# A new order table for block-sparse attention and a GELU MLP: loads in a fixed order, SyncE counted as held by its DMA ring, outputs from SyncE or GpSimd

## The chip, the cores and the metric

The kernel runs on one core of one Trainium2 chip. The metric is device time in microseconds for one execution, and a smaller number is better. The core has TensorE (matrix products, called PE in the profile), VectorE (DVE), ScalarE (ACT), GpSimd (POOL) and SyncE (SP). Each takes its own instructions in order; semaphores tie them together. SyncE computes nothing: it issues DMAs. Each DMA it issues here stands in the profile as an "SPq" instruction, whose length is the time SyncE was held by it.

## What is computed

For each of 4 batches and 8 heads, 768 queries of width 64 attend to keys in blocks of 64. A query picks 3 blocks by the product with the mean key of each block, and its own block, under a causal mask. The heads of a batch are then put side by side and go through a two-layer MLP with GELU.

```python
k_rep = k.reshape(B, H, n_blocks, 64, D).mean(axis=3)
gate_scores = np.einsum('bhsd,bhnd->bhsn', q, k_rep)        # causal blocks only
top_idx = np.argsort(gate_scores, axis=-1)[..., -3:]         # plus the own block
scores = scale * np.matmul(q, k.transpose(0, 1, 3, 2))       # masked to those, causal
attn = np.exp(scores) / np.sum(np.exp(scores), axis=-1)      # in short
x = np.matmul(attn, v)      # heads side by side: [3072, 512]
h = x @ w_in                # [512, 2048]
out = gelu_tanh(h) @ w_out  # [2048, 512]
```

## The kernel before

**Work.** Two heads of a batch make a pair, so there are 16 pairs, p = 0 to 15, and 4 pairs to a batch b. For each pair the kernel loads q, k and v (named q5, k5, v5 for pair 5), turns q and k, computes the gate, selects blocks with ten maximum instructions (`sel_e`), and turns the selection into a mask. The scores of a pair are made in six or seven units, written (pair, unit): a score product (`st_e`) into one of two wide PSUM buffers, an exponential on ScalarE (`ex_e`), a causal select on GpSimd (`af_e`), and a product with v (`pv_e`). A norm (`zr_e`) and a transpose (`ot_e` on TensorE, or `otd_e` by DMA) follow. When the four pairs of a batch are done, `s1` makes the first MLP product in 16 strips f with GELU, and `s2` the second in 6 output tiles ti of 16 matmuls each; `cp_e` copies a tile out of PSUM to one of four buffers (`NOSB`), and `out_e` sends it to memory. A tile that reuses a buffer waits until the tile four before it has landed. The second product of one batch is interleaved with the attention of the next.

**Order.** Nothing is scheduled on the chip. Each piece is an `Op` made with `add`: the engines it can run on with assumed times, a function that emits it, and what it depends on. `ORDER` (line 22) is a table, written out by hand or by a search, of the numbers of these operations in the order in which they are placed; a letter behind a number picks the engine where there is a choice. `Plan.place` (line 165) goes through it and gives each operation a planned start; the instructions are then emitted in the order of these starts. So on each engine, the order of the table is the order of the program. The assumed times decide nothing else. `Plan.spare` (line 200) puts spare matmuls with a zero tile into holes of the planned TensorE time (`zero_mm`, line 1276).

**Loads.** `load_half` (line 371) loads the first pair's q and k in halves, two DMAs each (line 378). `load` (line 328) loads the others: as two DMAs (line 346), or, for q and k from pair 4 on, as four in another layout (line 355) which VectorE then turns. q and k have four buffers each and v three, so k4 takes the buffer of k0. A small copy `keep` (line 1304) reads k0 late, and so holds k4 back. `load_w` (line 573) casts the weights while they are loaded, by GpSimd: w_in in two parts, once v2 is there, and w_out in one, once k4, q4 and k5 are there. Before the issue it copies one element of each of these loads (line 582), which makes it wait for them. Mask transposes by DMA (`mask_d`, line 838), transposes of attention outputs (`otd_e`, line 1159) and all outputs (`out_e`, line 1255) but half of the last tile stand in SyncE's queue together with the loads.

Of the kernel before, what the change touches and what calls it, by code (L numbers as in the profile page):

```python
# [15 lines left out]
HOLD = 0  # L16
MASKVAL = 28672.0
# [5 lines left out]
1 2A 13 9 15 0 30 8 31D 6 161 3 288A 5 10 12 26 16 18 39 19 21 27 32 33 40 34  # L23
43 14 59 92 56 61 94 22 89 95 125 57 62 122 58 24 44A 41A 28A 38D 76 77A 53 29
54 42 45 52 78 35 36A 160 51A 80A 37 162 46 47 48 49D 7 109 165 166 167 25 163
66 79 91 169 170 97 50 55 70 173 177 68A 75 128 307 127 64 124 310 130 309 312
67 71 72 110D 81 82 83 73A 174 178 74 69 111 113A 183 99 168 180 101A 184 181
100 190 171 84 287 175 164 85 103 117 112 86D 192 193 194 289 65 98 108 102 87
88 214 185 142 176 204 104 186 105 106D 143D 114 215 205 200 172 179 196 182
144 145 201 197 146A 115 116 191 208 187 107 118 132 119D 211 221 198 202 131  # L30
206 155 156 159 120 121 209 212 136 195 223 199 203 213 231 141 133 137 138
134D 139A 140 224 147 227 232 216 207 245 210 228 242 148 149 246 243 151 235
135 217 152D 218 153 229 225 150 233 236 237 157 188 239 226 230 222 252 240
154 158 254 255 219 258 259 260 256 303G 304 313 306 234 262 238 266 244 241
263 267 264 268 316 292D 248 189D 575 578D 220D 273 247 257 249 270 265 261 274
279 276 253 285 622 519 625 682 679 571 628 271 277 269 250 275 281 272 251D
278 354 355 339 280 283 284D 282A 356 357 340 341 342 315 322 358 343 286 317
384 385 386 387 624 521 627 388 334 335 336 337 394 395 396 397 338 374 375 376
377 398 523 524 580 528 344 345 346 347 378 348 318 319 320 321 323 379 380 381
382 576 527 579 4 349 350 351 352 581 582 533G 383 359 529 353 360 361 362 369  # L40
370 371 372 363 373 534G 530 583 531 532 296D 577D 324 325 326 327 328 329 330
331 332 364 535 333 525D 584 526A 365 366 367 389 368 390 391 392 393 537D 587
290 561 399 400 401 402 403 404 405 406 407 408 409 410 411 536D 545 588D 589D
538 539 632 634D 633 412 413 414 415D 636 635D 541 562 546 417 419 549 550 420
553 421 422 423 424 425 426 427 522 551 552 428 554 586A 291 547 301 555 557
637 684 681 590 573 429 558 585A 559 293 294 540 542 563 295 543 297 430 431
432 433 569 434 435A 437 548 638 439 440 639 694 640 641 591 441 592 593 600
560 442 443 444 445 604 446 447 601 605 544 612 556 564 448 449 450 596 451 452
453 689 642A 613 454 608 300D 690 693 643G 594 614 574 597 455A 609 630 644 940
937 645 646A 647A 457 459 460 461 462 463 695 692D 565 696 697 698 606 602 464  # L50
465 466 467 468 469 603 470 595 598 599 298 299 610 699G 631 657 658 620 942
939 701 685 702 687 648 471 653 654 655 616 566 472 473 474 611 669 570 691D
952 475D 703D 477 670 479 480 661 607 481 482 649 662 659 650 671 651 483 656
665 484 485 615 677 666 621 302 714 715 660 486 706 487 707 652 488 710 711
700G 947 617 704D 667 663 673 948 705 489 664 668 722 490 491 726 708 688 712
723 724 716 727 728 951 492 672 493 674 718 678 719 734 720 995 997 567 436 308
943 416 93 63 618 568 418 945 713 494 953 709 495A 497 742 717 729 725 721 735
499 500 501 502 503 504 505 1005 730 731 732 949D 733D 740 1008A 1006 954 675
456 998 619 676 736 737 738 506 739 1000 507 743 508 744 745 741 746 747 509
748 749 750 751 950A 757 758 759 760 761 957D 1010 1009 958G 1007D 812 1011 955  # L60
813 814 815 777 778 779 780 816 781 807 808 809 810 767 768 769 770 811 787 788
789 790 771 762 763 764 765 791 766 797 798 799 800 792 793 794 795 801 752 753
754 755 796 756 772 773 774 775 776 782 783 784 785 786 802 803 804 805 806 956
1012 1013 1109 1111 1119 1122D 1014 1112 1114 1124 1052 686 1054 1062 1120 999
1055 572 1110 1057 1067 959 960 961D 1123 962D 1121D 1063 123 1113 1367 314 438
1369 1017 1058 1368 1018 1066 969 1068 1069 1019D 510 1125 511 512 513 514 973
1126 1065D 1020D 1070 1127 1071 1016G 1060 515D 1015G 946G 623 476 1115 963 517
817 818 819 820 821 822 823 824 965 970 974 971 975 985 825 826 986 977 827 972
828 978 981 982 1061D 987 1072G 983 829 830 831 964 966 967 979 993 832 976
1021 458 833D 1064D 1128 1117 835 1030 1031 837 838 988 1034 984 1035 968 496  # L70
938 1001 1003 1074 1075 1076D 1004G 1077D 1056 1425 1427 498 478 1022 1023 839
980 840 1026 841 842 1042 1027 989 990 1130D 1435 1436 1036 1032 1043 1073G
1028 1044 1024 994 1033 843 844 1038 1039 1050 845 1037 1087 1078 846 1029 1088
847 848 849 850 1095 1096 1025 1045 1083 1040 1129D 1089 851 1084 1046 852 853D
855 857 858 1091 859 1041 1079 860 1092 861 1090 1099 862 863 1097 1085 1080
1100 1131 1132 1133D 864 865 1136 1428 1430 1377 1440 1439 1134D 1047 1081 1093
866 1086 1082 1107 1051 1137 1140 1141 1094 867 1144 868 869 870 1118G 1101
1145 1135 871 1152 1102 872 1153 1148 1098 1378 1103 1104 873D 1381 1149 875
1108 1146 1138 1150 1142 305 991 992 877 878 879 1156 1157 1164 1158 1154 880
881 882 883 884 885 1147 1139 1143 886 1159 1151 1155 1160 1161 1370 1372 1116  # L80
1373 680 1048 126 1053 1105 23 1375 1165 1166 1172 887 888 1049 1173 1106 1162
1167 1168 1382 1383 1163D 889 1169 1482 17 626 1484 890 1174 1175 891 892 1170
1171 1176 1187 1188 1189 1190 1379D 1191 1192 1193 1194 1195 1237 1238 1239
1441 1196 1240 1241 1242 1243 1244 1245 1232 1233 1234 1235 1246 1236 1217 1218
1219 1220 1221 1182 1183 1184 1185 1177 1178 1179 1180 1186 1181 1222 1223 1224
1225 1226 1197 1198 1199 1200 1201 1212 1213 1214 1215 1216 1207 1208 1209 1210
1437D 1380D 1438D 1384 1385 1386 1492 1539 1541 1549 1442 1443 1444 1485 1487
129 1431 1433 944 1389 1390 1392D 1550 1497 1495D 1493 1391D 1552D 1503G 1388D
1542 1483 520 516 518 1002 1544 1447 1486 629 1448 1488 854 1371 1374 1494D
893D 834 894 11 1387G 1376G 1545 874 1554 1560D 1553 1496 1227 1228 1229 1230  # L90
1211 1202 1203 1204 1205 1231 1206 1395 1411 1412 895 897 898 899 1555 1415
# [127 lines left out]
def kernel(  # L219
# [1096 lines left out]
    for p in range(HP, NPAIR):  # L1316
# [4 lines left out]
        if hp == HP - 1:  # L1321
            s1(b)
            s2(b)
# [37 lines left out]
```

## Time and profile before

| | us |
|---|---|
| median of 4 runs (lowest, highest) | 266.5 (265.65, 267.67) |
| the profiled execution | 265.66 |
| its span, first to last instruction | 264.0 |

The granted TensorE clock was 0.998 of full speed over the span. How the stretches that the change touches stand (us busy in each):

| stretch, us | PE | DVE | ACT | POOL |
|---|---|---|---|---|
| 0 to 43.6: loads, attention of batch 0 | 41.08 | 28.73 | 33.31 | 20.73 |
| 43.6 to 64.3: first MLP product of batch 0 | 20.35 | 11.53 | 12.87 | 3.87 |
| 64.3 to 97.4: second product, attention of batch 1 | 33.10 | 24.30 | 26.98 | 19.61 |
| 97.4 to 99.1 | 0.18 | 1.46 | 0.64 | 0.13 |
| 99.1 to 264: the rest | 161.22 | 76.64 | 94.75 | 31.62 |

In the profile's lists, the issues of DMAs with their sizes and the median time until they land:

```profile
slot_v<-in_v_dram SPq DMA_DIRECT2D x32, 192.0 KB, 4.0
out_dram<-slot_osb SPq DMA_DIRECT2D x23, 256.0 KB, 2.5
slot_q<-in_q_dram SPq DMA_DIRECT2D x52, 96.0 KB, 3.4
slot_k<-in_k_dram SPq DMA_DIRECT2D x52, 96.0 KB, 3.6
w_in<-in_moe_w_in_dram POOLq DMA_DIRECT2D x2, 1024.0 KB, 9.4
w_out<-in_moe_w_out_dram POOLq DMA_DIRECT2D x1, 2048.0 KB, 17.7
```

A line such as "PE bank L1229 <- DMA w_out" in the list of waits says that TensorE's instruction of line 1229, writing the tile `bank`, stood idle until that DMA landed. L1229 is the second MLP product, L1192 the first. A busy TensorE is not TensorE at its peak: matmuls overlap, so the time from one start to the next is the better measure of their rate.

### The profile page before, as it was taken

The page shows a single profiled execution, that of the slowest core. Times are in us where ns is not written, and L with a number is a line of the kernel's source. Part 1 is how long each engine was busy: PE and PEld are TensorE (multiplying, and loading weights), DVE is VectorE, ACT ScalarE, POOL GpSimd, SP SyncE. Part 2 cuts the span into 40 slices and gives each one's busy share as a digit, 9 for nine tenths or more (in the row PEclk, how much of TensorE's full clock was granted, in tenths as well). Part 3 has the DMA queues.
Part 4 walks back from the last instruction along what each step waited for, and adds up shares of the span by engine and source line. Part 5 has one row for each costly group of instructions (what it writes and reads, how often), then busy time and mean ns, then how long its engine had stood idle before and what let it go on. Part 6 is the DMA issues. An engine that isn't in the chain of part 4 may idle for free.

```text
span 264.0 us, 5782 instructions
## 1 busy us (share of the span) xinstructions
PE 255.9 (97%) x2243; PEld 148.4 (56%) x2243; DVE 142.7 (54%) x452; ACT 168.5 (64%) x216; POOL 76.0 (29%) x152
## 2 busy tenths in 40 slices
PE   8899999999999979999999999999999999999994
PEld 7556566655555655555566655555565655554441
DVE  3588873666577876982699697934942400002000
ACT  4688896658797966767888825677778355530020
POOL 5075750500358551200374300402554000000000
PEclk9999999999999999999999999999999999999999
DMA  5999999999957999999437689480231300100332
GB/s 124 230 204 192 154 197 158 155 199 168 154 116 122 150 222 180 143 121 249 86 59 129 135 137 173 95 264 0 50 74 32 109 2 0 48 34 0 140 138 79
DMA packets 133627, 33.14 MB, mean 126 GB/s; under 512 B 127328, under 2 KB 129632, under 8 KB 133600
## 3 DMA queue, kind: packets, MB, share of 16 engines
q1 hardware_dynamic: 130336, 28.46, 60.2%
q0 software_dynamic: 3120, 4.19, 9.7%
q8 instruction: 17, 0.28, 0.5%
q10 hardware_dynamic: 144, 0.13, 0.1%
q14 instruction: 10, 0.08, 0.1%
HBM read 27.26 MB, written 6.29 MB: 127 GB/s over the span
## 4 chain that ended last, share of the span: by engine, by line
PE 81%; DMA 9%; SPq 4%; DVE 2%; ACT 1%; issue 1%; POOL 1%; DVEq 0%; ACTq 0%; POOLq 0%
PE bank L1229 32%; PE wide L1192 24%; PE wide L1077 10%; DMA w_out<-in_moe_w_out_dram 7%; PE bank L1119 6%; PE wide L943 3%; SPq L355 2%; DMA slot_q<-in_q_dram 2%; PE bank L773 2%; SPq L378 1%; PE bank L991 1%; PE bank L398 1%; PE bank L684 1%; ACT slot_at L959 1%; POOL slot_at L975 0%
## 5 line engine op out<-in xcount | busy, mean ns | idle before, releaser
L1229 PE MATMUL bank<-w_out,slot_gT 128*128 128x512 f16 x384 | 100.3, 379 | 1.8 <-ACT slot_osb L302 1.5
L1192 PE MATMUL wide<-slot_xT,w_in 128*128 128x512 f16 (+1 forms) x512 | 89.0, 326 | 0.0
L1212 ACT ACTIVATE slot_gT<-wide 128x768 f16<-128x768 f32 x64 | 51.8, 810 | 41.0 <-PE wide L1192 41.0
L1091 ACT ACTIVATE slot_at<-wide 128x896 f16<-128x896 f32 x72 | 63.5, 915 | 14.2 <-PE wide L1077 11.0
L1192 PEld LDWEIGHTS <-w_in 128*128 128x128 f16 x512 | 49.2, 98 | 33.8 <-issue 1.0
L1229 PEld LDWEIGHTS <-slot_gT 128*128 128x128 f16 x384 | 35.9, 97 | 34.8 <-issue 3.7
L1104 POOL TENSOR_SCALAR_AFFINE_SELECT slot_at<-slot_at 128x256 f16<-128x256 f16 x72 | 30.1, 431 | 65.4 <-ACT slot_at L1091 62.9
L306 DVE COPY slot_osb<-bank 128x512 f32<-128x512 f32 (+1 forms) x14 | 9.3, 665 | 61.4 <-PE bank L1229 61.4
L1077 PE MATMUL wide<-qT,kT 76*128 76x512 f16 (+3 forms) x192 | 39.1, 305 | 0.0
L1077 PEld LDWEIGHTS <-kT 76*128 76x128 f16 x192 | 17.3, 98 | 16.1 <-issue 0.3
L1119 PEld LDWEIGHTS <-slot_at 128*128 128x128 f16 x504 | 21.6, 98 | 7.4 <-issue 0.5
L959 ACT ACTIVATE slot_at<-wide 128x768 f16<-128x768 f32 x28 | 22.4, 813 | 3.0 <-PE wide L943 1.5
L302 ACT COPY slot_osb<-bank 128x512 f32<-128x512 f32 (+1 forms) x11 | 6.2, 563 | 27.7 <-PE bank L1229 13.6
L1119 PE MATMUL bank<-v,slot_at 128*128 128x65 f16 x504 | 23.6, 194 | 0.0
L304 POOL CAST qT<-slot_qT 64x768 f16<-64x768 f32 (+1 forms) x17 | 14.6, 860 | 25.0 <-DVE slot_qT L695 17.4
L304 POOL CAST v<-slot_v 128x768 f16<-128x768 f32 x14 | 11.7, 843 | 15.9 <-DMA slot_v<-in_v_dram 15.9
L787 DVE STREAM_TRANSPOSE slot_gtT<-bank 128x160 f32<-128x160 f32 x15 | 5.2, 348 | 20.0 <-PE bank L773 18.4
L1140 DVE TENSOR_TENSOR slot_xn<-bank,slot_zr 128x384 f16<-128x384 f32 x24 | 13.4, 558 | 0.8
L695 DVE STREAM_TRANSPOSE slot_kT<-slot_k 128x768 f32<-128x768 f32 x12 | 11.5, 968 | 3.8 <-DMA slot_k<-in_k_dram 3.7
L695 DVE STREAM_TRANSPOSE slot_qT<-slot_q 128x768 f32<-128x768 f32 x12 | 11.5, 963 | 2.6 <-DMA slot_q<-in_q_dram 2.6
L803 DVE MAX8 slot_mx<-slot_gtT 128x8 f32<-128x12 f32 x150 | 12.3, 156 | 0.4
L975 POOL TENSOR_SCALAR_AFFINE_SELECT slot_at<-slot_at 128x512 f16<-128x512 f16 (+1 forms) x16 | 8.6, 550 | 12.0 <-ACT slot_at L959 11.9
(100 smaller groups left out, 221.7 us busy)
## 6 DMA issues: line engine op xcount, KB each, us to landing
slot_v<-in_v_dram SPq DMA_DIRECT2D x32, 192.0 KB, 4.0
out_dram<-slot_osb SPq DMA_DIRECT2D x23, 256.0 KB, 2.5
slot_q<-in_q_dram SPq DMA_DIRECT2D x52, 96.0 KB, 3.4
slot_k<-in_k_dram SPq DMA_DIRECT2D x52, 96.0 KB, 3.6
w_in<-in_moe_w_in_dram POOLq DMA_DIRECT2D x2, 1024.0 KB, 9.4
w_out<-in_moe_w_out_dram POOLq DMA_DIRECT2D x1, 2048.0 KB, 17.7
slot_q<-in_q_dram SPq DMA_DIRECT2D x6, 192.0 KB, 3.9
slot_k<-in_k_dram SPq DMA_DIRECT2D x6, 192.0 KB, 4.4
```

The lines of the kernel that those rows point to most:

```text
L304: nc.gpsimd.tensor_copy(out=out, in_=in_)
L695: nc.vector.transpose(out=T[key + "T32", p], in_=T[key, p].rearrange("p t j -> p (t j)"))
L803: nc.vector.max(out=mx8[:, x, :], in_=T["gtT", p][:, :, 0:NBLK][:, x, :])
L959: nc.scalar.activation(out=bass.AP(at.tensor, at.offset, [at.ap[0], [512, 2], [1, HALF]]), in_=plan.buf["st", u].rearrange("p (h w) -> p h ...
L1077: nc.tensor.matmul(st[:, x:e], kT16[i][h][0:76, jc * 128:jc * 128 + 128], qT16[i][h][0:76, qa * 128 + (x - cb): qa * 128 + (e - cb)], star ...
L1091: nc.scalar.activation(out=T["at", u][:, 0:n], in_=plan.buf["st", u][:, 0:n], func=AF.Exp, bias=0.0, scale=SCALE)
L1104: nc.gpsimd.affine_select(out=dg, in_=dg, compare_op=ALU.is_ge, fill=0.0, base=0, pattern=[[0, dcount], [1, 128]], channel_multiplier=-1)
L1119: nc.tensor.matmul(pvv[:, qc, 0:65], at[:, x:x + 128], v16[i][:, jc, h, :], start=first and k_ == 0, stop=k_ == len(todo) - 1, skip_group_ ...
L1140: nc.vector.tensor_tensor(out=T["xn", p][:, :, h, :], in0=pvv[:, :, 0:64], in1=zr.to_broadcast([128, NC, 64]), op=ALU.mult)
L1192: nc.tensor.matmul(hps[:, u:e], w_in16[:, ci, f * 128:(f + 1) * 128], T["xT", b][:, ci, u:e], start=(ci == 0), stop=(ci == HP - 1))
L1212: nc.scalar.activation(out=T["gT", b][:, f, :], in_=plan.buf["hps", b, f][:, 0:S], func=AF.Gelu_apprx_tanh, bias=0.0, scale=1.0)
L1229: nc.tensor.matmul(plan.buf["ops", b, ti], T["gT", b][:, f, ti * 128:(ti + 1) * 128], w_out16[:, f, :], start=(f == 0), stop=(f == NF - 1))
```

## The change

The order table is new throughout, and so are the numbers in it, because some operations are gone: where SyncE's time for a load was a 0.1 us operation with an empty one of 1.0 or 1.9 us behind it, it is now one operation of 1.1 or 2.0. Other assumed times change with it. A list `LOADS` fixes the order of the loads, as dependences of the planner. An output of batches 0 to 2 is issued by SyncE or by GpSimd, as a letter in the table says (S or G). The number of spare matmuls allowed, and how long and how densely they are planned, change too.

```diff
+LOADS = """k1 q1 v0 k2 q2 v1 k3 q3 v2 v3 q4 k4 k5 q5 v4 k6 q6 v5 k7 q7 v6 k8 q8 v7
+k9 q9 v8 k10 q10 v9 k11 q11 v10 v11 k12 q12 v12 k13 q13 v13 k14 q14 v14 k15 q15
+v15"""
...
 ORDER = """
-1 2A 13 9 15 0 30 8 31D 6 161 3 288A 5 10 12 26 16 18 39 19 21 27 32 33 40 34
...
+0 10 11 21 12 13 25 16 14 51 53 6 18 4 3 1 2A 7 5 26D 22 17 38 23A 39D 27 15
...
-                d = 0.111 if at < slow else 0.058
+                d = 0.1 if at < slow else 0.05
...
-        go = add({SP: 0.1}, emit_t if dve else emit, deps, prio=order)
-        add({SP: 1.9 if dve else 1.0}, lambda _: None, [go], prio=order)
+        go = add({SP: 2.0 if dve else 1.1}, emit_t if dve else emit, deps,
+                 prio=order)
+        load_go[f"{key}{p}"] = go
...
-        go = add({SP: 0.1}, emit, [], prio=order - 200)
-        add({SP: 0.95}, lambda _: None, [go], prio=order - 200)
-        ld[key, 0, a] = add({"DMA": 0.9}, lambda _: None, [go], prio=order)
+        go = add({SP: 1.05}, emit, [], prio=order - 200)
+        halves0.append(go)
+        ld[key, 0, a] = add({"DMA": 0.05}, lambda _: None, [go], prio=order)
...
-            m = add({SP: 0.6}, mask_d, [sel] + free.get(("mk", p - 1), []),
+            m = add({SP: 1.2}, mask_d, [sel] + free.get(("mk", p - 1), []),
...
-            ot = add({SP: 0.6}, otd_e, norms + s1_all.get(b - 2, []), base - 20)
+            ot = add({SP: 1.2}, otd_e, norms + s1_all.get(b - 2, []), base - 20)
...
-                    (nc.scalar if eng == ACT else nc.sync).dma_start(
+                    {ACT: nc.scalar, POOL: nc.gpsimd}.get(
+                        eng, nc.sync).dma_start(
...
-                go = add({ACT if parts == 2 and x == 0 else SP: 0.1}, out_e,
+                go = add({SP: 0.6, POOL: 1.1} if b < B - 1 else
+                         {ACT if parts == 2 and x == 0 else SP: 0.6}, out_e,
                          [cp], 1000 * b + 500)
...
-            osb_free.append(add({"NONE": 2.5}, lambda _: None, [go],
+            osb_free.append(add({"NONE": 3.0}, lambda _: None, [go],
                                 1000 * b + 500))
...
+    before = [None, None, None]
+    prev = halves0
+    for name in LOADS.split():
+        go = load_go[name]
+        go.deps += [d for d in prev + before[:1] if d is not None]
+        prev = [go]
+        before = before[1:] + [ld[name[0], int(name[1:])]]
     order = [(op.start, lambda op=op: op.emit(op.eng))
              for op in plan.place(ORDER)]
-    order += plan.spare(bank, zero_mm, 110, 42.0, 4.4)
+    order += plan.spare(bank, zero_mm, 300, 30.0, 4.4)
```

Read by what each number stands for, SyncE's queue begins as follows (a and b are the halves of the first pair; waits and transposes for later pairs are left out):

| | SyncE's order |
|---|---|
| before | q0a k0a k0b q0b q1 q2 k1 v0 k2 v2 q3 v1 k3 v3 q4 k5 k4 q5 k6 v4 q6 q7 k7 v5 v6, mask of pair 6, q8 k8, mask of pair 7, v7 k9, transpose of pair 4, output 1, v8, output 0, transposes of pairs 5 and 6, output 2 |
| after | k0a q0a q0b k0b k1 q1 v0 k2 q2 v1 k3 q3 v2 v3 q4 k4 k5 q5 v4 k6 q6 v5 k7 q7, mask of pair 6, v6 k8 q8, mask of pair 7, transpose of pair 4, outputs 0 and 2, v7, transpose of pair 5, k9, transpose of pair 6 |

Six outputs go through GpSimd (tiles 1 and 5 of batch 0, 0 and 2 of batch 1, 2 and 3 of batch 2). Between the first and the last exponential of batch 0, ScalarE has four other copies where it had six. `keep` runs on VectorE, where it ran on GpSimd. The matmuls other than the spare ones are the same.

## The prediction

> **What bounds the kernel now.** I read the busy times first, then what TensorE waited for, then the chain of waits in order of time, and at last the timeline around two places that the chain names.
>
> The page's busy row:
>
> ```profile
> PE 255.9 (97%) x2243; PEld 148.4 (56%) x2243; DVE 142.7 (54%) x452; ACT 168.5 (64%) x216; POOL 76.0 (29%) x152
> ```
>
> The group of spare matmuls (busy us, mean ns), and then TensorE's longest waits (us in total, times, longest):
>
> ```profile
> L1276 PE MATMUL bank<-z 128*128 128x128 f16 x57 | 6.9, 267 | 1.1 <-DVE bmask L263 1.1
> ```
>
> ```profile
> PE bank L1229 <- ACT slot_osb L302: 1.5, 1, 1.5
> PE bank L684 <- DMA slot_q<-in_q_dram: 0.8, 1, 0.8
> PE bank L1229 <- DMA w_out<-in_moe_w_out_dram: 0.3, 1, 0.3
> ```
>
> The reader is to see that TensorE is the bound, and that an order table can save little: every useful matmul stays. Start to start, the 57 spare ones (L1276, which fill planned holes) take 5.7 us, and the gaps over 150 ns add up to 4.9 us. About 10 of 264 us are in play, about 8 of them before 43.6 us.
>
> The chain of waits in order of time (start, us, what) shows which holes are real:
>
> ```profile
> 36.68 0.14 POOL slot_keep L304
> ...
> 37.96 2.72 SPq L355
> ...
> 40.72 2.66 SPq L355
> ...
> 43.43 2.33 DMA slot_q<-in_q_dram
> ...
> 46.59 17.67 DMA w_out<-in_moe_w_out_dram
> ...
> 64.30 2.96 PE bank L1229 x13
> ...
> 97.88 0.57 DVE slot_xn L1140
> 98.45 0.59 ACT slot_osb L302
> 99.08 1.67 PE bank L1229 x7
> ```
>
> Two things carry the end of the run. First, w_out: GpSimd issues it at 46.59, once k4, q4 and k5 are there, and the second product of batch 0 cannot start before 64.26. TensorE reaches that point at about 63.8, so the two are level: **whatever is won before it is lost again unless w_out comes earlier**. Second, the hole at 97.4 to 99.1. ScalarE's copy at 98.45 is of output tile 4 of batch 0; it reuses the buffer of tile 0, whose output SyncE issued only at 93.66 and which landed at 98.35. After 64.3 us nothing else holds TensorE for over 0.15 us: all later work is at its rate.
>
> **The change, part by part.** Edits with one answer: the planner's new durations (SyncE 1.1 or 2.0 per load, 0.6 or 1.2 per output or transpose, 3.0 for a buffer) and the list LOADS enter only as times and dependences of the planner; they emit nothing. What runs is the new table: I read it engine by engine, by what each number stands for. The spare matmuls may be 300 instead of 110, placed up to 30 us instead of 42, 0.05 us apart; warm ones take 0.053, so they overshoot a filled hole by at most 6% of some 6 us: 0 to 0.4 us, taken as 0.1 within the start.
>
> **Start.** Halves of k and q of pair 0 now go k, q, q, k (before: q, k, k, q), and k1 goes ahead of q1 and q2. I put the new loads into the landing times that the trace has for the same places in SyncE's queue: first halves at 3.58, 4.73, 5.97, 6.95, then k1 at 9.00, q1 10.79, v0 12.61. By the rows: first k transposes 3.7 to 4.9, q to 5.5, second q 6.1 to 6.5, gate to 6.9, second k 7.1 to 8.1; VectorE selects (0.97 us) from 8.4; mask 9.5 to 9.75; k1 transposes to 10.2, and ScalarE's mask copy (0.37) beside them; score matmuls 10.4 to 10.85; first exponential 11.1. Before it was 11.69: the 0.8 us wait for q1 (L684), in front of the first mask, is gone; the second k half is late next. Gain 0.6 us.
>
> **Attention of batch 0.** ScalarE runs the exponentials nearly back to back from 26.9 to 39.7, so its copies count. Between the first and last exponential it had six of 0.48 us, now four (the others are VectorE's, which has room at 28.7 of 43.6 us): 1.0 us. The last exponential ends near 38.1 instead of 39.7. Two copies of attention outputs (0.8 and 0.5) now follow it with the table load (1.5), to 40.9, beside the norm and transposes that took as long before: 0. So the first product is in flow from 42.1 instead of 43.6 and, after the 20.1 us it took, ends at 62.2.
>
> **w_out.** The price is in these rows of the timeline (start, us, engine, line, what):
>
> ```profile
> 28.48 0.92 POOL L584 DMA_DIRECT2D w_in<-in_moe_w_in_dram  x1 [0.31 <-POOL w_in L582]
> ...
> 33.38 0.76 POOL L584 DMA_DIRECT2D w_in<-in_moe_w_in_dram  x1
> ...
> 36.84 6.54 SPq L355 DMA_DIRECT2D slot_k<-in_k_dram  x4
> ...
> 43.43 2.32 SPq L355 DMA_DIRECT2D slot_q<-in_q_dram  x4
> ```
>
> A transposed load is four DMAs, 2.3 us of SyncE when free; k4 took 6.5 because w_in, landing at 43.60, held its ring. The table changes three things. (1) w_in goes earlier: v2 takes the ninth place among the whole loads (landing 24.0 instead of 18.9), then its cast (0.83), a memset behind the last score product of pair 1, and 0.5 of marker and issue give 25.9 instead of 28.5; the second half comes near 30 instead of 33.4. The two took 15.1 us from first issue to last landing, so w_in ends near 41.0, not 43.6. (2) The copy "keep", which k4 waits for, moves from GpSimd (36.7) to VectorE behind the first norm of pair 2: near 33.9. As w_in still blocks the ring, this frees SyncE but not k4. (3) k5 was issued at 26.4, ahead of k4; now it stands **behind** k4, and w_out waits for both. So k4 is through at 41.0, k5 takes 2.3, the last part lands 2.7 later (q5's did) at 46.0, the marker copy and issue take 0.5: w_out goes at 46.5, before 46.59, and lands at 64.2. The 2.6 us won on w_in pay for k5. Bounds: 2.0 earlier if w_in drains at 39; 2.5 later if it ends at 43.6 as before. I take 0.1 earlier, the row-by-row sum. TensorE then stands from 62.2 to 64.2: all of the earlier gain is lost here.
>
> Here a rule weighs in. The Trainium skill, "TensorE: Matmul & The Clock Gate" (What's actually happening), puts the array at half clock after an idle window of about 3.4 us. The granted clock is 1.00 in every stretch asked for, across the 1.7 us hole too, and no later hole is longer; only the first 24 spare matmuls came 0.109 us apart, against 0.053 later. By the row a 2.0 us stall costs itself; by the rule too, but one of 4.6 us (w_out 2.5 late) would add up to 1.7 us of slow matmuls. I take nothing, and keep the 1.7 for the slow end.
>
> **Outputs and later batches.** In the new SyncE queue output 0 stands right behind the mask of pair 7 and one transpose, ahead of v7; tile 1 goes through GpSimd. The mask waits for VectorE's selection of pair 7, which ends near 85.5; output 0 then goes at about 88 and lands by 90.5 (out_dram's median is 2.5), and the copy of tile 4 comes near 95. So the hole at 97.4 goes: 1.7 us. Late next would be otd of pair 6 (its attention output's transpose), needed at 100.8 and landing near 98. Six outputs move to GpSimd. One costs SyncE 0.33 to 0.58 us; GpSimd's own issues cost 0.76 to 1.17. That is 6 x 1 us on an engine 29% busy, and behind an output stand causal selects (0.43 each) that TensorE needs only some us later: 0. Against this move speaks the skill, "SBUF — State Buffer" (SBUF: two separate sides): descriptors of a GpSimd DMA are written through the port it shares with VectorE, and a DMA of 0.62 us took 3.1 beside a VectorE copy. No row here shows it. By the rule each of the six lands about 2.5 us later. The tightest reuse is tile 3 of batch 2, whose buffer takes tile 1 of batch 3: 4.5 us by the rows, 7 by the rule, against some 9.5 us of matmuls (44 of 0.217) before the bank is needed. Nothing either way; if that cover were gone, 0 to 2.5 us each.
>
> Batches 1 to 3 have TensorE full before, so there is no gain, only new holes to fear. Checked by hand, pair 6's gate comes near 72.9 with its operands at 71.8; others have more room. The tail has the same split copies and issues: 0.
>
> **Sum.** From the profiled 265.66 us (span 264.0 and 1.7 around it): w_out 0.1, the hole 1.7, in all 1.8, so 263.9. The runs' median is 266.5, 0.8 above that execution; in its terms **264.7 us**.
>
> **Rivals.**
> *w_out early.* If w_in drains by 39, w_out lands at or before 62.2, and TensorE keeps 2.0 more: 262.7. For it: less k and q traffic falls into w_in's time. Against: q4 and v3 do.
> *k5 decides (slower).* If w_in ends at 43.6 as now, because two 1 MB casts share the DMA engines with v3 and q4, w_out lands 2.5 later: with the hole gone +0.8, with the slow clock +2.5: 267.3 to 269. It decides once w_in ends later than about 42.9, where the loss exceeds 1.7.
> *New holes later.* One or two of the kind at 97.4 in another batch (a mask on SyncE with loads behind it, a bank not free) give back 1.7 to 3.5: 266.4 to 268.2.
> *Nothing happens:* the planner's figures emit nothing, but every queue's order changes, so I give this no share of its own.
>
> **Numbers.** Forecast 0.38 (its own range 263.8 to 265.8), w_out early 0.17, k5 decides 0.20, new holes 0.25. Changes of under 0.5% (1.3 us) can't be told from none. Faster: most of the first and all of the second, 0.50; same 0.22; slower: most of the last two, 0.28. The range runs into both sides: 262.3 to 268.6.
>
> **What would show it.** In the new profile: first exponential near 11.1; w_in landing near 41; w_out issued near 46.5; TensorE waiting about 2 us for w_out; no wait of L1229 for slot_osb near 97. Wrong if w_out is issued before 45 or after 48, or if a wait of over 1 us stands after 64.

## The result and the profile after

| | before | after |
|---|---|---|
| median, us | 266.28 (52 runs) | 264.56 (33 runs) |
| ratio, 95% interval | | 0.9946 (0.9934 to 0.9959) |
| profiled execution, us | 265.66 | 264.78 |
| its span, us | 264.0 | 263.1 |
| last matmul starts, us | 259.94 | 258.83 |

The forecast was 264.7, so the sum came out. Its terms did not all come out, and the two profiles are 0.9 us apart where the medians are 1.7. Some matmuls that the two profiles share, in us from the start:

| | before | after | forecast |
|---|---|---|---|
| first score product | 10.53 | 11.82 | 10.4 |
| first exponential | 11.69 | 12.36 | 11.1 |
| last exponential of batch 0 ends | 39.68 | 41.08 | 38.1 |
| last matmul of s1(0) | 63.06 | 64.45 | 62.2 |
| first matmul of s2(0) | 64.30 | 64.95 | 64.2 |
| first matmul of s2(0) to last matmul of all | 195.64 | 193.88 | 193.9 |

The start, forecast to gain, lost 0.7 to 1.4 us in this pair. Executions of one start differ by some tenths: with the start of the kernel before, s1(0) begins at 40.12 here and at 40.58 in b_out0 below; with the start of the kernel after, at 41.53 here and at 41.06 to 41.22 in the four runs below that leave it alone (a_split, a_wout5, a_outSP, a_out0late). So the loss is between 0.5 and 1.4. The later part gained 1.76, as forecast, and that figure is steady: the eight profiles below that leave output 0 at its new place have 193.88 or 193.89 too. The difference of 1.1 in the last matmul is the sum of 0.65 lost up to s2(0) and 1.76 won behind it.

The page's busy row, and the group of spare matmuls (busy us, mean ns, idle before), of the kernel after:

```profile
PE 257.5 (98%) x2300; PEld 151.1 (57%) x2300; DVE 145.0 (55%) x459; ACT 165.2 (63%) x208; POOL 80.2 (30%) x159
...
L1281 PE MATMUL bank<-z 128*128 128x128 f16 x114 | 10.3, 243 | 1.1 <-DVE bmask L263 1.1
```

There are 57 more matmuls, all spare ones. From start to start they take 8.8 us instead of 5.7. TensorE looks busier, but with work nobody reads.

TensorE's list of waits after (us in total, times, longest) is short:

```profile
PE bank L1281 <- DVE bmask L263: 1.1, 1, 1.1
PE bank L401 <- DVE slot_qT L306: 0.4, 1, 0.4
```

The wait for `slot_osb` (1.5) and the one for q1 (0.8) are gone, and so is the small one for w_out. GpSimd's timeline around the weights (start, us, engine, line, what, idle time before and its releaser):

```profile
26.55 0.94 POOL L587 DMA_DIRECT2D w_in<-in_moe_w_in_dram  x1 [0.31 <-POOL w_in L585]
...
31.85 0.77 POOL L587 DMA_DIRECT2D w_in<-in_moe_w_in_dram  x1
...
43.73 0.18 POOL L585 CAST w_out<-slot_k 1x1 f16<-1x1 f32 x1 [2.82 <-DMA slot_k<-in_k_dram]
43.85 0.18 POOL L585 CAST w_out<-slot_q 1x1 f16<-1x1 f32 x1
47.49 0.18 POOL L585 CAST w_out<-slot_k 1x1 f16<-1x1 f32 x1 [3.45 <-DMA slot_k<-in_k_dram]
47.97 1.18 POOL L587 DMA_DIRECT2D w_out<-in_moe_w_out_dram  x1 [0.30 <-POOL w_out L585]
```

The markers of k4 and q4 are through at 44.0. The third, k5's, waits until 47.49 for the last part of k5, and w_out goes at 47.97, 1.4 later than before. It lands at 64.91. SyncE's timeline shows k5's issue, and q5's behind it:

```profile
41.20 2.36 SPq L357 DMA_DIRECT2D slot_k<-in_k_dram  x4
43.60 3.91 SPq L357 DMA_DIRECT2D slot_q<-in_q_dram  x4
```

TensorE's timeline where w_out lands:

```profile
64.95 1.89 PE L1232 MATMUL bank<-w_out,slot_gT 128*128 128x512 f16 x8
```

The second product starts 0.04 us behind the landing, and the list shows no wait: TensorE and w_out arrive together. That is so in this execution: in a_outSP below, with the same start, w_out lands at 65.44 and TensorE waits 0.7 us for it; in a_out0late it lands at 63.41, 1.1 us ahead of need. SyncE's timeline around output 0, before and then after, shows where the later gain lies:

```profile
93.66 0.54 SPq L1255 DMA_DIRECT2D out_dram<-slot_osb  x1
```

```profile
87.93 1.24 SPq L1162 DMA_TRANSPOSE slot_xT<-slot_xn  x1
89.22 1.05 SPq L1259 DMA_DIRECT2D out_dram<-slot_osb  x2
90.37 1.08 SPq L348 DMA_DIRECT2D slot_v<-in_v_dram  x2
```

Outputs 0 and 2 go at 89.2 and 89.9, ahead of the load of v7. Output 0 lands at 91.53; the copy of tile 4 (now VectorE's) runs at 95.89, and there is no hole at 97. From 64 us on TensorE stands nowhere for more than 0.15 us.

### The profile page after: what moved, and what is told of

It is laid out like the page before. It is cut to its first block, busy times and chain, and to the rows that moved or that the text cites. A ratio compares the mean times of both kernels' runs of the same rounds, so it can differ in the third digit from the quotient of the medians.

```text
span 263.1 us, 5902 instructions
## 1 busy us (share of the span) xinstructions
PE 257.5 (98%) x2300; PEld 151.1 (57%) x2300; DVE 145.0 (55%) x459; ACT 165.2 (63%) x208; POOL 80.2 (30%) x159
## 4 chain that ended last, share of the span: by engine, by line
PE 98%; DVE 1%; issue 0%; ACT 0%; DVEq 0%
PE wide L1195 32%; PE bank L1232 32%; PE wide L1080 10%; PE bank L1122 6%; PE wide L946 5%; PE bank L1281 3%; PE bank L994 2%; PE bank L776 2%; PE bank L401 1%; PE bank L399 1%; PE bank L687 1%; PE bank L1036 1%; PE bank L835 1%; PE bank L1153 0%; PE bank L467 0%; PE bank L489 0%
## 5 line engine op out<-in xcount | busy, mean ns | idle before, releaser
L1195 PE MATMUL wide<-slot_xT,w_in 128*128 128x512 f16 (+1 forms) x512 | 89.9, 326 | 0.1
L1107 POOL TENSOR_SCALAR_AFFINE_SELECT slot_at<-slot_at 128x256 f16<-128x256 f16 x72 | 30.8, 438 | 62.5 <-ACT slot_at L1094 62.2
L306 DVE COPY slot_osb<-bank 128x512 f32<-128x512 f32 (+1 forms) x15 | 10.1, 672 | 62.3 <-PE bank L1232 38.0
L304 POOL CAST qT<-slot_qT 64x768 f16<-64x768 f32 (+2 forms) x21 | 17.0, 809 | 16.2 <-DVE ksb L735 12.0
L302 ACT COPY slot_osb<-bank 128x512 f32<-128x512 f32 (+1 forms) x10 | 5.6, 565 | 25.8 <-PE bank L1232 25.8
L304 POOL CAST v<-slot_v 128x768 f16<-128x768 f32 x12 | 10.0, 836 | 28.6 <-DMA slot_v<-in_v_dram 28.5
L1259 POOL DMA_DIRECT2D out_dram<-slot_osb x6 | 3.4, 566 | 36.2 <-ACT slot_osb L302 36.2
L1142 DVE RECIPROCAL slot_zr<-bank 128x6 f32<-128x6 f32 x24 | 4.5, 189 | 15.7 <-PE bank L1122 15.7
## 6 DMA issues: line engine op xcount, KB each, us to landing
w_out<-in_moe_w_out_dram POOLq DMA_DIRECT2D x1, 2048.0 KB, 16.9
```

What stands on the lines that cost most here:

```text
L304: nc.gpsimd.tensor_copy(out=out, in_=in_)
L1107: nc.gpsimd.affine_select(out=dg, in_=dg, compare_op=ALU.is_ge, fill=0.0, base=0, pattern=[[0, dcount], [1, 128]], channel_multiplier=-1)
L1195: nc.tensor.matmul(hps[:, u:e], w_in16[:, ci, f * 128:(f + 1) * 128], T["xT", b][:, ci, u:e], start=(ci == 0), stop=(ci == HP - 1))
```

## The experiments

Each was timed against runs of the kernel before on the same chip; a ratio is to that kernel. Where an edit shortens the printed table by a line, line numbers are one lower than in the kernel it comes from; the split of w_out makes those behind it one higher.

### Where the later gain comes from

**b_out0**, the kernel before with one number moved:

```diff
-... 939 701 685 ... 943 416 93
+... 939 701 416 685 ... 943 93
```

> The kernel before with one token moved: SyncE issues output 0 of batch 0 right behind the mask transpose at 85.5 us (issue near 86.9 instead of 93.66); nothing else differs. Theory A, the hole at 97.4-99.1 came from that output's landing and is all that the change gained: output 0 lands near 89.5, ScalarE's copy of tile 4 comes at 96.2-97 instead of 98.45, TensorE's stall of 1.5 us is gone, and the time falls by 1.3-1.8 us (ratio 0.993-0.995), as much as the whole change or a little more since this kernel's w_out lands at 64.26. Rival D, the gain of the change came from elsewhere (the new order of loads, GpSimd's outputs): another wait takes the hole's place, time within 0.5 us of the kernel before (ratio 0.998-1.001).

Measured: 265.11 us median against 266.04, ratio 0.9959 (0.9938 to 0.9981). Output 0 was issued at 88.17 and landed at 90.59. The long waits of TensorE that are left:

```profile
PE bank L683 <- DMA slot_q<-in_q_dram: 1.9, 1, 1.9
...
PE bank L1228 <- DMA w_out<-in_moe_w_out_dram: 0.7, 1, 0.7
PE wide L1191 <- DMA w_in<-in_moe_w_in_dram: 0.5, 1, 0.5
```

No `slot_osb`. In this execution q1 landed later, w_out landed at 65.56, and s2(0) started at 65.61; from there to the last matmul it took 194.12 us against 195.64. The hole is gone, and 1.5 us with it. The time fell by 0.9 us (0.4%), less than the 1.3 to 1.8 of theory A; that the hole came from this output holds, and rival D falls.

**a_out0late**, the reverse in the kernel after:

```diff
-... 548 398S 438S 660 ... 966 400
+... 548 438S 660 ... 966 398S 400
```

> The changed kernel with output 0 of batch 0 issued later by SyncE, behind the k load at 95.5 us (issue near 96 instead of 89.22); nothing else differs. Theory A, its place on SyncE is the change's whole gain: it lands near 98.5-99, ScalarE's copy of tile 4 waits for it, TensorE stands 1.0-2.0 us there, and the time rises by 1.0-2.0 us (ratio to the kernel before 0.998-1.002). Rival D, the gain came from elsewhere: time within 0.4 us of the changed kernel (ratio 0.993-0.996).

Measured: 266.22 us, ratio 1.0016 (0.9991 to 1.0041): one output at another place in a queue gives back all that the change brought. VectorE's timeline, and then the chain of waits in order of time (start, us, what):

```profile
98.69 0.69 DVE L305 COPY slot_osb<-bank 128x512 f32<-128x512 f32 x1 [3.13 <-DMA out_dram<-slot_osb]
99.29 0.17 DVE L734 TENSOR_TENSOR ksb<-bmask,slot_ks 128x24 f32<-128x24 f32 x1
```

```profile
95.17 3.42 DMA out_dram<-slot_osb
...
98.69 0.13 DVE slot_osb L305
...
99.29 0.19 DVE ksb L734
...
99.52 0.48 PE bank L775 x8
```

The hole has another cover here than in the kernel before. There ScalarE's copy came late and TensorE lacked the buffer; here VectorE's copy stands 3.1 us, the small product `ksb` is queued behind it, and TensorE's gate product lacks that. The profiled execution was one of the shortest of its runs (265.41) and shows 0.9 us of it; the median rose by more, 1.7. Between 0.9 and 1.7 the profile doesn't say what else there is. Theory A holds for the later part, though the copy that waits is VectorE's and not ScalarE's; rival D falls.

**b_three** is the kernel before with output 0 moved, 26 spare matmuls and w_out in two halves (both edits are shown below).

> The kernel before, its own order table, with three edits: output 0 issued behind the mask transpose at 85.5 us, 26 spare matmuls, w_out as two halves. Theory A, these three are all that there is to gain and the rest of the new table is worth nothing: 263.0-264.0 us, ratio 0.988-0.992, level with the changed kernel with the same two edits (263.2 us), and TensorE has no wait over 1 us after 40 us. Rival, the new order of loads is itself worth something: 264.2-265 us (ratio 0.993-0.997), since s1(0) ends 0.5-1.5 us later than the 62.91 of the changed kernel with those edits.

Measured: 265.76 us, ratio 0.9967 (0.9932 to 1.0002). The rival was right, and by more than it said: 265.76 against its 264.2 to 265. TensorE's waits of over 1 us after 36 us:

```profile
PE wide L1192 <- DMA w_in<-in_moe_w_in_dram: 1.2, 1, 1.2
PE wide L1192 <- DMA slot_xT<-slot_xn: 1.2, 1, 1.2
```

w_in lands at 44.43 (43.60 in the kernel before), and s1(0) waits for it; the new table has it at 41.2. Later, output 0 has landed at 91.47, but the transposes of pairs 5 and 6 (`otd_e`) are issued at 96.00 and 97.34, land at 101.23 and 101.74, and s1(1) waits for them. The new table issues them at 91.54 and 96.13; they land at 96.38 and 100.03, and none is late. In b_out0 they landed at 100.68 and 101.33, nearly as late, and nothing waited: s2(0) had started 1 us later there. So output 0 is the first wait in line; behind it stand the transposes, which show only when TensorE comes early enough, and the new table has both.

### GpSimd's outputs

**a_outSP** turns the six back: `418G 808G 498G 848G 1266G 1286G` become `418S 808S 498S 848S 1266S 1286S`.

> The changed kernel with its six GpSimd outputs issued by SyncE, at the same places of the order table. Theory A, GpSimd's outputs cost nothing and gain nothing: each lands some 0.5-1 us sooner after its issue, no wait of TensorE over 0.5 us comes or goes, time within 0.3 us of the changed kernel (ratio 0.993-0.996). Rival: SyncE's queue is what the change unloads, so that loads, mask transposes and outputs behind them come later: time up by 0.5 us or more (ratio over 0.997), with a wait of TensorE or ScalarE on an output tile or a transposed tile that the changed kernel lacks.

Measured: 264.33 us, ratio 0.9934 (0.9907 to 0.9962), no change. In the kernel after the page's table of DMA issues has (count, KB each, median us to landing):

```profile
out_dram<-slot_osb SPq DMA_DIRECT2D x17, 256.0 KB, 2.3
...
out_dram<-slot_osb POOLq DMA_DIRECT2D x6, 256.0 KB, 3.2
```

GpSimd's land 0.9 us later than the other 17, but they also stand at places where outputs land later: issued by SyncE in a_outSP, the same six land 2.0 to 3.5 us after their issue, median 2.8 against 3.2. VectorE stands 8.1 us at the end for one of them (issued at 239.63, landed at 241.91), TensorE for none. The forecast that no wait over 0.5 us comes was missed: in this execution TensorE waits 0.7 us for w_out, which took 17.6 us to land. No output had been issued by then.

### w_out

**a_wout5** takes one marker away:

```diff
-                            [("k", HP), ("q", HP), ("k", HP + 1)], 1, 400)
+                            [("k", HP), ("q", HP)], 1, 400)
```

> The changed kernel with pair 5's k taken out of the tile reads that hold the load of w_out, and nothing else. Theory A, w_out is what s2(0) starts on, and k5 holds it: w_out is issued at 44-45.5 us instead of 47.97 and lands at 62-63.5 instead of 64.91; TensorE then comes to s2(0) at its own time, 64.7, so the time falls by 0.1-0.3 us only (ratio 0.993-0.995). Rival B, k5's last pieces share the DMA engines with w_out: w_out lands at 64-65 whenever it is issued, k5 lands several us later than 47.44, time within 0.2 us. Rival C, the transposes of k5 come late and hold the pair-5 scores: time up by 0.5 us or more.

Measured: 275.17 us, ratio 1.0328 (1.0298 to 1.0359), the worst of all, and no theory had its size. w_out did go earlier, at 44.89, and landed at 60.65. But then (TensorE's waits, and SyncE's timeline):

```profile
PE bank L776 <- DVE slot_qT L698: 9.6, 1, 9.6
```

```profile
44.41 7.31 SPq L357 DMA_DIRECT2D slot_q<-in_q_dram  x4
```

q5's four parts are issued at 44.41 to 51.73 where they took 3.9 us after the change; its last three parts are issued behind w_out, and the last lands at 61.84, against 49.87. Its turned form feeds the gate of pair 5, which stands inside s1(0) in TensorE's order, so TensorE stood until 63.00. So k5's marker is not only a wait that holds w_out: it lets q5, next in SyncE's queue, get to the DMA engines ahead of w_out. Rival C had the mechanism but named k5, and allowed for 0.5 us or more.

The stall shows the clock as well. TensorE's last matmuls ahead of it, and then stretches of this run (stretch and its length, busy us and count of TensorE, weight loads, VectorE, ScalarE, GpSimd; then granted clock, DMA share, GB/s):

```profile
51.63 1.80 PE L1195 MATMUL wide<-slot_xT,w_in 128*128 128x512 f16 x10
```

```profile
55.00:55.50 0.50, 0.00 (x0) 0.00 (x0) 0.00 (x0) 0.00 (x0) 0.00 (x0) 1.00 1.45 219
55.50:56.00 0.50, 0.00 (x0) 0.00 (x0) 0.00 (x0) 0.00 (x0) 0.00 (x0) 0.57 1.46 220
56.00:63.00 7.00, 0.00 (x0) 0.00 (x1) 1.03 (x2) 0.00 (x0) 0.00 (x0) 0.50 1.40 202
63.00:65.50 2.50, 2.50 (x14) 1.06 (x15) 2.33 (x16) 0.30 (x1) 0.00 (x0) 0.50 0.98 145
...
66.00:68.00 2.00, 2.00 (x18) 1.34 (x17) 0.77 (x3) 0.82 (x2) 0.00 (x0) 1.00 1.09 168
```

**a_both** also limits the spare matmuls to 26, the edit of the next part.

> Both edits. Theory A: w_out lands at 61.5-63 us, s1(0) ends at 63.4-64.0, s2(0) starts at 63.6-64.2 against 64.95 in the changed kernel, and the time falls by 0.8-1.4 us against it (ratio to the kernel before 0.989-0.992): more than the two edits one by one. Rival B: no more than 0.3 us (ratio 0.993-0.996).

Measured: 274.52 us, ratio 1.0317 (1.0278 to 1.0356): the same stall (9.1 us), so both forecasts fail. It is 0.65 us under a_wout5, with ranges that overlap.

**a_split** loads w_out as two DMAs, one behind the other, so that the first eight matmuls of a tile need the first half only:

```diff
-                nc.gpsimd.dma_start(out=dst[:, :, x * w:(x + 1) * w],
-                                    in_=view[:, :, x * w:(x + 1) * w])
+                for y in ([slice(0, n)] if name == "in" else [slice(0, n // 2), slice(n // 2, n)]):
+                  nc.gpsimd.dma_start(out=dst[:, y, x * w:(x + 1) * w],
+                                    in_=view[:, y, x * w:(x + 1) * w])
```

(The marker loop's own `n` is renamed, so that `n` keeps the number of chunks.)

> The changed kernel with w_out loaded as two transfers of 1 MB, feature chunks 0-7 and 8-15, one behind the other. Theory A, in the changed kernel TensorE comes to s2(0) just as w_out lands (64.7 against 64.91), since the spare matmuls hold it up earlier: the first half lands near 56 us, s2(0) starts at 64.6-64.8, and the time falls by 0-0.3 us (ratio to the kernel before 0.993-0.995). Rival, w_out's landing alone sets s2(0): start at 63.5 or earlier, time down by over 1 us (ratio below 0.991).

Measured: 264.36 us, ratio 0.9947 (0.9927 to 0.9967), no gain. The first half landed at 59.0, later than expected, the second at 64.5, and s2(0) started at 64.56, 0.5 us behind the end of s1(0), as in the kernel after. With the data there TensorE still comes at 64.6: in this execution it is the start, not w_out, that sets s2(0).

### The spare matmuls

**a_spare26** keeps the 26 in front of the first transpose:

```diff
-    order += plan.spare(bank, zero_mm, 300, 30.0, 4.4)
+    order += plan.spare(bank, zero_mm, 26, 30.0, 4.4)
```

> The changed kernel with its spare matmuls limited to the 26 ahead of the first transpose (114 before). Theory A, spares stand in front of ready work: the first score moves from 11.82 us to 10.8-11.3, the first exponential from 12.36 to 11.4-11.9, the last matmul of s1(0) from 64.45 to 63.4-64.0; exponential 18 releases SyncE earlier by the same, so w_out lands at 64.0-64.5 instead of 64.91, s2(0) starts at 64.0-64.5 instead of 64.95 and the time falls by 0.5 to 1.0 us against the changed kernel (ratio to the kernel before 0.991-0.993). Rival B, the spares stand in gaps that are empty anyway, and keep TensorE's clock up: first score not earlier than 11.6, matmuls of the first 12 us no shorter or longer than before, time within 0.3 us of the changed kernel or above it (ratio 0.994-0.997).

Measured: 263.78 us, ratio 0.9903 (0.9875 to 0.9932), 0.8 us better than after by the medians. TensorE's timeline between 4 and 12 us, of the kernel after and then of this one:

```profile
4.18 1.64 PE L399 MATMUL bank<-idb,slot_k 128*128 128x130 f32 x6
...
6.47 0.93 PE L1281 MATMUL bank<-z 128*128 128x128 f16 x13
7.24 0.50 PE L467 MATMUL bank<-idb,slot_q 128*128 128x128 f32 x3
...
10.49 1.06 PE L1281 MATMUL bank<-z 128*128 128x128 f16 x16
11.39 0.50 PE L401 MATMUL bank<-idb,slot_k 128*128 128x128 f32 x3
11.82 0.28 PE L946 MATMUL wide<-qT,kT 64*128 64x256 f16 x2
```

```profile
3.90 0.92 PE L399 MATMUL bank<-idb,slot_k 128*128 128x130 f32 x6
...
5.88 0.52 PE L467 MATMUL bank<-idb,slot_q 128*128 128x128 f32 x3 [0.44 <-DMA slot_q<-in_q_dram]
...
9.11 0.52 PE L401 MATMUL bank<-idb,slot_k 128*128 128x128 f32 x3
9.55 0.28 PE L946 MATMUL wide<-qT,kT 64*128 64x256 f16 x2
```

The planner saw holes there, and the chip had none: in the kernel after the second half of q had landed at 5.93, and k1 at 9.15, while spare matmuls ran. In these two profiles the first score is 2.3 us earlier, more than theory A said, and s1(0) ends 1.9 earlier, but s2(0) starts at 64.33, only 0.6 earlier, because now it does wait for w_out, landed at 64.28:

```profile
64.33 1.89 PE L1232 MATMUL bank<-w_out,slot_gT 128*128 128x512 f16 x8 [1.14 <-DMA w_out<-in_moe_w_out_dram]
```

Part of the 2.3 us has another cause. The first six transposes (L399) took 1.64 us in the kernel after and 0.92 here, though both have the same 26 spare matmuls ahead of them: one follows the other by 0.21 us there, and by 0.11 here. In the kernel after the pace doubles between 6.3 and 6.6 us, and the trace's first record of the granted clock stands at 6.54; here it stands at 3.93, where the two programs do not differ yet. In five executions of the start of the kernel after it stands at 4.37, 5.28, 5.94, 6.08 and 6.54. So this part isn't the edit's doing. Two runs whose first clock records stand together, both without k5's marker, make a fairer pair:

| us | a_wout5, 114 spare | a_both, 26 spare |
|---|---|---|
| first record of the clock | 4.37 | 4.29 |
| first score | 10.79 | 9.61 |
| first exponential | 11.33 | 10.63 |
| 20th exponential | 32.85 | 31.16 |
| s1(0) starts | 41.06 | 39.44 |

So the spare matmuls cost the first score 1.2 us, and the start of s1(0) 1.6.

**a_spare26_split** has the 26 spare matmuls and the two halves.

> 26 spare matmuls and the two halves of w_out. Theory A: with the spares gone TensorE stood 1.1 us for w_out in the run with 26 spares; that wait goes, s1(0) ends at 62.3-62.8, s2(0) starts at 62.9-63.4 instead of 64.33, and the time falls by another 0.9-1.2 us (262.6-262.9 us, ratio to the kernel before 0.986-0.988). Rival: the second half lands later than 65 us, or the issue on GpSimd delays its casts; TensorE waits in the middle of the first output tile and no more than 0.4 us is gained over 26 spares alone (ratio 0.989-0.991).

Measured: 263.2 us (262.84 to 263.39), ratio 0.9901 (0.9876 to 0.9927), 1.2 us below a_split, which ran beside it. s2(0) starts at 63.40, the 1.14 us are gone, as theory A said; the time lies between the two forecasts, with the rival's ratio. The second half landed at 65.15, but no matmul waited for it. Alone the halves bring nothing that can be told. Here they bring 0.6 us by the medians, but a_spare26 ran on another chip, and the ratios (0.9903 and 0.9901) don't tell the two apart: the gain of the halves shows in the profile alone.

**a_spare0_split** has no spare matmul at all (`zero_mm, 0, 30.0, 4.4`).

> The changed kernel with no spare matmul at all, and w_out as two halves; against the run with 26 spares and the halves. If the 26 at the start warm TensorE up: granted clock below 0.9 in the first 10 us, the fp32 transposes of the first k take up to twice their 0.1 us each, the first score comes 0.3-1.5 us later than 9.71, and the time rises by 0.2-1.0 us (263.4-264.2). If the clock is granted anyway: clock 1.00 from the first matmul on, time 263.2 within 0.3 us.

Measured: 263.17 us (262.78 to 263.42), ratio 0.9872 (0.9838 to 0.9905), the same as with 26: of each forecast one half came, slow transposes and a late first score, but no loss of time. Its timeline of the first transposes:

```profile
4.38 1.64 PE L399 MATMUL bank<-idb,slot_k 128*128 128x130 f32 x6 [4.38 <-POOL E L609]
...
7.82 1.67 PE L399 MATMUL bank<-idb,slot_k 128*128 128x130 f32 x6
...
10.74 0.50 PE L401 MATMUL bank<-idb,slot_k 128*128 128x128 f32 x3
11.17 0.28 PE L947 MATMUL wide<-qT,kT 64*128 64x256 f16 x2
```

Up to 9 us a transpose follows the one before by 0.21 us where it was 0.11 in a_spare26, and the first score comes at 11.17, 1.5 later than with 26. Yet the last exponential of batch 0 ends at 39.12, against 39.08. So my account of a_spare26 was too simple: the first score is not what holds s1(0). The starts of some exponentials of batch 0:

| | after | a_spare26 | a_spare0_split | a_spare79 |
|---|---|---|---|---|
| first | 12.36 | 10.43 | 12.19 | 11.85 |
| 12th | 25.41 | 23.54 | 23.94 | 24.37 |
| 20th | 33.32 | 30.93 | 31.36 | 31.76 |
| 28th | 40.26 | 37.97 | 38.31 | 38.71 |

Without spares the lead over the kernel after grows from 0.2 to 2.0 us between the first and the 20th. There stand the 35 spare matmuls that the kernel after has between 12.7 and 34 us; at 0.053 each that is 1.9. a_spare26 brings a lead of 1.9 to this stretch, and at the 12th it is no larger: its chain of waits goes through SyncE's loads to q3, which lands at 22.16. At the 20th it is 2.4.

**a_spare79** keeps all spare matmuls ahead of the first score and drops those 35 (`zero_mm, 79, 30.0, 4.4`).

> The changed kernel with the first 79 of its 114 spare matmuls, so with all that stand ahead of the first score, and without the 35 that stand between 12.7 and 34 us. If the spares ahead of the first score are what holds s1(0) (the theory of the run with 26 spares): first exponential near 12.3, s1(0) starts at 41.0-41.5, time within 0.2 us of the changed kernel (264.3-264.7). If it is the late 35, each with its 0.053 us on the in-order path of TensorE (the theory formed on the run with none, whose first score at 11.17 still had s1(0) at 39.58): first exponential as late, near 12.3, but exponential 20 at 31.3-31.6 instead of 33.32, s1(0) starts at 39.4-39.9, s2(0) at w_out's landing near 64.2-64.6, and the time falls by 0.5-0.9 us (263.6-264.0, ratio 0.989-0.993).

Measured: 264.21 us (263.2 to 265.94), ratio 0.995 (0.9915 to 0.9985). In the profile the lead grows from 0.5 at the first exponential to 1.6 at the 20th, s1(0) starts at 39.98 instead of 41.53, and s2(0) at 63.57. That is for the late 35, at some 1.0 us of the 1.9 expected. The time doesn't decide: its runs spread over 2.7 us, those of the kernel after lie mostly within 0.7. The other profiles help, since by s1(0) the early differences have shrunk: it starts at 41.06 to 41.53 in the five with all 114, at 39.98 with 79, at 39.23 to 39.53 in the three with 26, and at 39.58 with none. So the late 35 cost 1.1 to 1.5 us, the 53 between the first transpose and the first score 0.4 to 0.8, and the first 26 nothing. With 79 there is one profile only, so this division is rough.

**b_spare26** is the same limit in the kernel before (26 for 110; of its 57 spare matmuls 26 stay, 24 of them ahead of its first transpose).

> The kernel before with its spare matmuls limited to the 26 ahead of the first transpose (57 before), nothing else. Theory A, spares in front of ready work cost the start: the first score stays at 10.2-10.6 us (the new order of loads without them has it at 9.55), w_out lands at 63.7-64.3 instead of 64.26, s2(0) starts on it, and the time falls by 0-0.5 us (ratio 0.998-1.000): here w_out binds and few spares stood in front of ready work. Rival, the start is the same in both tables once the spares are gone: first score below 10.0, ratio below 0.997.

Measured: 265.94 us, ratio 0.9982 (0.9951 to 1.0013); first score at 10.58, w_out landed at 62.60, s2(0) at 63.90. No change that can be told, as expected; but s2(0) did not start on w_out, which had landed 1.3 us before. With 26 spares each, the new order has its first score at 9.55 to 9.71 in three profiles, the old one at 10.58 here and 11.11 in b_three. The clock was recorded later in those two (5.45 and 6.94, against 3.93 to 4.29), so not all of these 0.9 to 1.6 us is the order of the loads. At s1(0) 0.2 to 0.8 us are left (39.23 to 39.53 against 39.77 and 39.98): that much of a gain by the new order of the loads was hidden behind the spare matmuls.

## Why the prediction was right, step by step

The time was right to 0.1 us, and part of that is luck. The sum took 1.8 us off the profiled 265.66 and came to 263.9; the profiled execution of the kernel after took 264.78, so in the profiles the sum is 0.9 us too good. The forecast then added 0.8, by which the median of 4 runs stood above their profile. After the change the median stands 0.2 under its profile, and so the median fell by 1.7 where the profiles fell by 0.9.

- **Outputs (1.7): right.** Output 0 was issued at 89.2 (forecast 88) and landed at 91.5 (90.5); the hole went, and 1.76 us between s2(0) and the end. Moved alone, this output brings 0.4% to the old kernel and takes 0.6% from the new one. The step named the transpose of pair 6 as late next: it landed at 100.03, not 98, and nothing waited. b_three shows that the transposes of pairs 5 and 6 are next in line indeed, and that the new table covers both.
- **Six outputs on GpSimd (0): right.** 0.57 us of issue each, 0.4 later to land by the medians than the same six from SyncE, no change in time.
- **The planner's figures (nothing): right for the useful work, wrong for the spare matmuls.** Worked out from the code, with no run: with `LOADS` and SyncE's new durations taken back, every engine's other instructions come out the same, but some 80 spare matmuls are placed instead of 114. So these figures do put work on TensorE, through `Plan.spare`.
- **w_in: right.** Issued at 26.55 and 31.85 (forecast 25.9 and 30), landed at 41.17 (41.0).
- **w_out (0.1 gained): the mechanism right, the size 0.75 off, and it would have been more.** k5 did take its place behind k4, with 41.2 to 43.6 for its issue, but its last part landed at 47.44, not 46.0: 3.9 us behind the end of its issue, where I had taken q5's 2.7. Why it took longer is open. The marker and the issue then took 0.5, as forecast, and w_out went 1.5 us later than forecast. Half of that came back by luck: it landed 16.9 us later, where the sum had 17.7. Lost 0.65 instead of 0.1 won. That `keep` ran at 36.87, not near 33.9, cost nothing: k4's issue ended at 41.10, just as w_in landed.
- **Start (0.6 gained) and attention of batch 0 (the last exponential at 38.1): wrong.** The term that failed is "0 to 0.4 us, taken as 0.1" for the spare matmuls. I priced how far they overshoot a hole, not whether the planned hole is there. They delayed the start of s1(0) by 1.6 us in the two pairs that can be compared (a_wout5 and a_both, a_split and a_spare26_split), and by 2.3 between the kernel after and a_spare26. Without them the new order is ahead of the step at the first score (9.55) and 0.7 us behind it at the last exponential (38.78). The saving of 1.0 us by fewer copies on ScalarE didn't come even there: from first to last exponential it took 28.3 us, before 28.0. Its chain of waits goes through q3's load; that this is the reason is not shown.
- **TensorE stands 2.0 us for w_out: wrong for this kernel, right in kind.** Since TensorE came 2.3 us later than I had it (64.45 against 62.2), it met w_out without a wait, and the error in the start cost little: what the start was to gain was to be lost to w_out anyway. So one error hid the other. With 26 spares the stall is there, 1.1 us.

Of the five signs that the prediction named, two came (w_in's landing, no wait for `slot_osb`). Three did not: the first exponential came at 12.36, there was no wait for w_out, and w_out was issued at 47.97, just inside the 48 beyond which the forecast was to count as wrong. Two of its readings of the profile before were off: the gaps over 150 ns add up to 4.1 us in the list of waits, not 4.9, on which nothing rests; and the clock's row at 1.00 says nothing of the start, since the trace's first record of the clock stands at 6.92.

Of the rivals, *w_out early* didn't happen. *k5 decides* happened with a quarter of its size: w_in ended early, as the forecast had it, and k5's landing alone gave 0.65. *New holes later* didn't: none is left after 64 us.

The rule on idle time that the prediction weighed (half clock after an idle window of about 3.4 us; the Trainium skill, "TensorE: Matmul & The Clock Gate", What's actually happening) had no place in the changed kernel, but a_wout5 shows it in kind. The last matmul ends at 53.43, and the trace has the clock at 0.50 from 55.57 to 65.81: it falls after 2.1 us, sooner than the page has it, and is back 2.8 us after the first new matmul. The gate product and the 12 matmuls behind it took 3.7 us where they take 2.4 in the kernel after: 1.3 us, near the 1.7 that the prediction kept as the most. The rule on GpSimd's descriptors (the Trainium skill, "SBUF — State Buffer", SBUF: two separate sides) would, by an estimate from its two durations, have outputs land 2.5 us later; measured 0.4 to 0.9.

## What to carry to other kernels

Work that fills planned holes costs nothing only where the hole exists on the chip: check in the profile whether the data for the next real instruction had landed before each filler ran. A wait that seems to hold a big transfer back for nothing may keep the queue behind it short; before it is taken away, ask which loads would then stand behind 2 MB, and what is queued behind them. And where two things arrive together, what mending one of them brings is cut off by the other: by the medians the split of w_out brought 0.2 us alone (not to be told from none), the limit on spare matmuls 0.8 alone, and both 1.4. On one chip, the limit brought 1.2 us to the kernel with the split. The changed kernel with both runs in 263.2 us, 1.0% under the kernel before and 0.5% under the changed one.

## What was not expected of the hardware

- While w_out's 2 MB came in, a DMA on SyncE took up to 9.2 us to issue (a load of k in a_split, at 50.85; 8.1 in the kernel after), where the median is 0.5, and loads landed up to 16 us after their issue, where the median is 3.7.
- Two halves of w_out, issued 0.9 us apart on one queue, landed at 59.0 and 64.5: the first took 11.4 us of the 16.9 of both.
- The clock's row reads 1.00 from the first matmul on in the run without spare matmuls, though transposes come 0.21 us apart until 9.1 us and 0.12 from 10.7 on. The trace has no record of the clock there before 9.50, and the row counts a stretch without a record as 1.00. With 26 matmuls ahead of the first transpose, the first record stands anywhere from 3.93 to 6.54.
- Runs of the old table, whatever was changed in it, spread over 2.2 to 3.9 us; those of the new one over 0.6 to 3.0, mostly under 1.8. Nothing here explains it.
